# Batch 1 of a fused attention and FFN kernel: projections one step sooner, q turned one or two steps sooner, score groups moved to two and one steps later

## The chip, the cores and the metric

The kernel runs on one core of one Trainium2 chip. A core has five engines that run their own instruction streams and meet at semaphores: PE (matrix multiply, with PEld for its weight loads), DVE (VectorE), ACT (ScalarE), POOL (GpSimd) and SP (SyncE). PE, DVE, ACT, POOL and SP execute their instructions in the order in which the program gives them; DMA transfers are issued by SP, ACT and POOL and run on 16 DMA engines. The metric is device time in microseconds, the median of several runs.

## The reference

Linformer attention for 8 batches of 8 heads, 1024 rows, head size 64, followed by a feed-forward network whose hidden layer is the maximum of three products:

```python
k_proj = np.einsum('ks,bhsd->bhkd', E, k)          # E, F: 64 x 1024
v_proj = np.einsum('ks,bhsd->bhkd', F, v)
scores = scale * np.matmul(q, k_proj.transpose(0, 1, 3, 2))
attn = softmax(scores)                              # over 64 columns
x = np.matmul(attn, v_proj)  -> (8192, 512)
h = np.maximum(np.maximum(x @ w1, x @ w2), x @ w3)  # 512 -> 768
out = h @ w_out                                     # 768 -> 512
```

Softmax is written there with the row maximum subtracted; the kernel computes the exponentials, their sums (by a product with ones) and the reciprocal as exp(-ln(sum)).

## The kernel before

The weights stay in the on-chip memory. Everything is worked out batch by batch: the attention of batch b + 1 is put between the steps of the FFN of batch b, by hand. All of PE's results go to one PSUM tile `ps` of eight banks: banks 0 to 3 rotate through the FFN (`fbank`), banks 4 to 7 belong to the attention.

**The FFN.** A batch has two halves (`ch`) of 512 tokens. A half has 18 layer-1 steps (`l1`): for each of six blocks of hidden units the products with w1, w2 and w3, four matmuls of 128x512 each (L188). ScalarE copies the first product to `h1s` (L191), VectorE takes the maximum with the second into `m12` (L193) and with the third into `hT` (L195). Then come four `down` steps (L212) of six matmuls, a ScalarE copy (L214) and a store from POOL (L219).

**Steps and groups.** After each step `tick()` counts `slot` up and calls the groups of the next batch's attention whose slot is reached. Groups stand in a list, in the order in which they are called. In batch 0 the first half is special (`l1_first`, `down_half`: slots 1 to 16), the second half gives slots 17 to 34 (one per layer-1 step), and its four down steps slots 35 to 38. So step 20 here is the layer-1 step that brings `slot` to 20; steps 17, 20, 23, 26, 29, 32 are those with the ScalarE copy.

**The attention of batch 1** has these groups:

- `g1[0]`, kv: 16 matmuls project k and v (L119, L121) into bank 4; ScalarE casts the result to `kp` (L126), VectorE repeats it (L127), SP issues a transposing DMA from `kp` to `kpT` (L176), ScalarE and VectorE write `vp` (L129, L130).
- `q_flip(1, 0..3)`: VectorE turns q, two heads at a time, from `q_t` to `qT` (L99).
- `g1[1]`, `g1[2]`, scores: 32 small matmuls each (L140) of `kpT` with four heads of `qT` into banks 4 to 7, then two exponentials on ScalarE into `pT` (L145), four banks in a call. Both groups use the same four banks, and each fills half of the columns twice over (gg = 0 and 1).
- `g1[3]`, sums: 16 matmuls of `pT` with ones (L154) and two logarithms (L161); `g1[4]`, `g1[5]`: reciprocals (L164); `g1[6]`, `g1[7]`: the products of `pT` with `vp` (L154), which VectorE multiplies by the reciprocals into `xT` (L169), the FFN's input.

**The loads.** POOL issues k, v and q of batch 1 early (L417 to L419); they run behind the weights. At slot 22 of batch 0 `load_behind_turn(2, "kvq")` makes POOL copy one element of `kpT` (L91), which waits for the transposing DMA, and then issues the loads of batch 2 (L87).

The other batches use the list that `attention` returns (kv at 2, scores at 10 and 15, sums at 20, and so on); batch 1 has the list of its own that the change touches.

Of the kernel before, what the change touches and what calls it, by code (L numbers as in the profile page):

```python
# [16 lines left out]
def kernel(ctx: ExitStack, tc: tile.TileContext, q, k, v, E, F, w1, w2, w3, w_out, out):  # L17
# [71 lines left out]
    def load_behind_turn(b, order="qkv"):  # L89

        nc.gpsimd.tensor_copy(out=seen, in_=kpT[(b - 1) % NB][:, 0, 0, 0:1])  # L91
        for c in order:
            load(b, *{"q": (q, q_t), "k": (k, k_t), "v": (v, v_t)}[c])
# [3 lines left out]
    def q_flip(b, g):  # L97
        hs = slice(2 * g, 2 * g + 2)
        nc.vector.transpose(  # L99
            out=qT[b % NB][:, hs].bitcast(FP32).rearrange("p h n -> p (h n)"),  # L100
            in_=q_t[b % NB][:, hs].rearrange("p h si d -> p (h si d)").bitcast(FP32),
        )
# [82 lines left out]
    def l1(b, ch, c, jt, i):  # L185
        bank = fbank()
        for ct in range(NCT):
            nc.tensor.matmul(out=ps[:, bank, :], lhsT=w_sb[i][:, ct, jt * P:(jt + 1) * P],  # L188
                             rhs=xT[b % 2][:, ct, ch, :], start=(ct == 0), stop=(ct == NCT - 1))
        if i == 0:  # L190
            nc.scalar.copy(out=h1s[jt % 2], in_=ps[:, bank, :])  # L191
        elif i == 1:
            nc.vector.tensor_tensor(out=m12[jt % 2], in0=ps[:, bank, :], in1=h1s[jt % 2], op=ALU.max)  # L193
        else:
            nc.vector.tensor_tensor(out=hT[c % 2][:, jt, :], in0=ps[:, bank, :], in1=m12[jt % 2], op=ALU.max)  # L195

    def down(b, ch, c, tt):
        o = o_acc[c % 2]
        if c == 2 * B - 1 and tt == 3:

            n = DO // 2
            for x, tmp in enumerate(h1s):
                bank = fbank()
                for jt in range(NJT):
                    nc.tensor.matmul(out=ps[:, bank, :n], lhsT=hT[c % 2][:, jt, tt * P:(tt + 1) * P],
                                     rhs=wo_sb[:, jt, x * n:(x + 1) * n], start=(jt == 0), stop=(jt == NJT - 1))
                (nc.scalar.copy if x else nc.vector.tensor_copy)(out=tmp[:, :n], in_=ps[:, bank, :n])
                (nc.scalar if x else nc.sync).dma_start(out=out_v[b, ch][:, tt, x * n:(x + 1) * n], in_=tmp[:, :n])
            return
        bank = fbank()  # L210
        for jt in range(NJT):
            nc.tensor.matmul(out=ps[:, bank, :], lhsT=hT[c % 2][:, jt, tt * P:(tt + 1) * P],  # L212
                             rhs=wo_sb[:, jt, :], start=(jt == 0), stop=(jt == NJT - 1))
        nc.scalar.copy(out=o[:, tt, :], in_=ps[:, bank, :])  # L214
        if c == 2 * B - 1:
            nc.sync.dma_start(out=out_v[b, ch][:, tt, :], in_=o[:, tt, :])
        elif tt % 2 == 1:
            dst = out_v[b, ch] if b else out_0[ch]
            nc.gpsimd.dma_start(out=dst[:, tt - 1:tt + 1, :], in_=o[:, tt - 1:tt + 1, :])  # L219

    def down_half(tt, x):

        bank = tt
        for jt in range(3 * x, 3 * x + 3):
            nc.tensor.matmul(out=ps[:, bank, :], lhsT=hT[0][:, jt, tt * P:(tt + 1) * P],  # L225
                             rhs=wo_sb[:, jt, :], start=(jt == 0), stop=(jt == NJT - 1))
        if x:
            nc.scalar.copy(out=o_acc[0][:, tt, :], in_=ps[:, bank, :])
            if tt % 2 == 1:
                nc.gpsimd.dma_start(out=out_0[0][:, tt - 1:tt + 1, :], in_=o_acc[0][:, tt - 1:tt + 1, :])  # L230


    def quads0(ch, bank, lhs, hhs=(0, 1)):
        for hh, j, g, u in QUADS:
            if hh not in hhs:
                continue
            rows = slice(u * KP, (u + 1) * KP)
            nc.tensor.matmul(out=ps[j * HD:(j + 1) * HD, bank + hh, :], lhsT=lhs(rows, g),  # L238
                             rhs=pT[rows, g, ch, :], start=True, stop=True, tile_position=(u * KP, j * HD))
# [24 lines left out]
    def sums0(ch, bank):  # L264
        quads0(ch, bank, lambda rows, g: ones[rows, :])
        nc.scalar.activation(out=lns[ch], in_=ps[:, bank:bank + 2, :], func=AF.Ln)
        nc.scalar.activation(out=rinv[ch], in_=lns[ch], func=AF.Exp, scale=-1.0)
# [30 lines left out]
    def av_up0():  # L298
        for f, bank in enumerate((6, 4)):
            quads0(1, bank, lambda rows, g: vp2[0][rows, g, f, :])  # L300
        norm0(1, 0, 6, (0, 1))
        norm0(1, 1, 4, (0, 1))
# [96 lines left out]
    def l1_first(i, jts, banks, between=None):  # L399
        for hh in range(2):  # L400
            if hh and between:
                between()
            for jt, bank in zip(jts, banks):
                for ct in (2 * hh, 2 * hh + 1):
                    nc.tensor.matmul(out=ps[:, bank, :], lhsT=w_sb[i][:, ct, jt * P:(jt + 1) * P], rhs=xT[0][:, ct, 0, :],  # L405
                                     start=(ct == 0), stop=(ct == NCT - 1))
                if hh:
                    nc.vector.tensor_tensor(out=h1c[jt] if i == 1 else hT[0][:, jt, :], in0=ps[:, bank, :], in1=h1c[jt],
                                            op=ALU.max)
                    yield  # L410
# [35 lines left out]
    for b in range(B):  # L446
        groups = attention(b + 1, turn_dma) if b + 1 < B else []
        if b == 0:
            g1 = [g for _, g in groups]
            groups = [(9, scores_up0), (12, lambda: sums0(1, 4)), (20, g1[0]),  # L450
                      (22, lambda: q_flip(1, 0)), (23, lambda: q_flip(1, 1)), (25, g1[1]), (26, lambda: q_flip(1, 2)),
                      (27, lambda: q_flip(1, 3)), (28, g1[2]),
                      (31, g1[3]), (32, g1[4]), (33, g1[5]), (34, g1[6]), (36, g1[7])]
        slot = 0
        gi = 0

        def tick():
            nonlocal slot, gi
            slot += 1
            while gi < len(groups) and groups[gi][0] <= slot:  # L460
                groups[gi][1]()
                gi += 1
            if b == 0:
                if slot == 22:
                    load_behind_turn(2, "kvq")
                return
            if b == 1 and slot in (4, 5, 6, 7):
                q_flip(2, slot - 4)
            if b + 2 < B:
                if slot == 9:  # L470
                    load_behind_turn(b + 2)
                if slot in (32, 34, 36, 38):
                    q_flip(b + 2, slot // 2 - 16)

        for ch in range(2):
            c = 2 * b + ch
            if c == 0:
                for part in ((1, range(6), (6, 7, 0, 1, 4, 5)), (2, range(3), (2, 3, 0), q_up0), (2, range(3, 6), (1, 2, 3))):
                    for _ in l1_first(*part):
                        tick()  # L480
                state["f"] = 3
                for x in range(2):
                    if x:
                        av_up0()
                    for tt in range(4):
                        down_half(tt, x)
                        if x:
                            tick()
                continue
            for s in range(18):  # L490
                l1(b, ch, c, s // 3, s % 3)
                tick()
                if pend and s in (2, 5, 8, 11):
                    pend.pop(0)()
                    tick()
            pend = [lambda tt=tt, b=b, ch=ch, c=c: down(b, ch, c, tt) for tt in range(4)]
        if b == 0:
            while pend:
                pend.pop(0)()
                tick()  # L500
# [32 lines left out]
```

The softmax here doesn't subtract the row's maximum and nothing guards it: scores larger than these inputs give would overflow.

## Time and profile before

| | |
|---|---|
| median of 8 runs | 400.9 us (400.51 to 401.11) |
| the profiled execution | 400.91 us |
| its span, first to last instruction | 399.0 us |
| PE busy | 388.1 us, 97% of the span, 2686 instructions |
| DVE busy | 200.2 us, 50% |
| ACT busy | 163.5 us, 41% |
| POOL busy | 66.6 us, 17% |
| chain that ended last | PE 92%, DVE 3%, DMA 2%, issue 1%, ACT 1% |

A busy PE counts the length of overlapping matmuls, so 97% says that PE seldom stands still and not how fast it works. The page's slices give the granted TensorE clock as 9 in all 40 of them, and its mean is 1.000. The stretch from 44.98 us (the first layer-1 matmul of batch 0's second half) to 73.21 us (the first of batch 1) is the one in which batch 1's attention is worked in. Busy time of the engines there, by stage:

| from to, us | what PE does | PE busy | DVE busy | ACT busy |
|---|---|---|---|---|
| 44.98 to 48.53 | steps 17 to 20 | 3.55 | 1.05 | 1.31 |
| 48.53 to 50.38 | kv | 1.85 | 0.33 | 0.58 |
| 50.38 to 55.51 | steps 21 to 25 | 4.44 | 4.15 | 1.53 |
| 55.51 to 58.79 | first scores, steps 26 to 28 | 3.23 | 1.41 | 2.42 |
| 58.79 to 63.11 | second scores, steps 29 to 31 | 3.49 | 1.89 | 2.42 |
| 63.11 to 66.37 | sums, steps 32 to 34 | 3.21 | 1.40 | 2.57 |
| 66.37 to 69.62 | product with vp, steps 35 and 36 | 3.25 | 3.15 | 2.33 |
| 69.62 to 73.21 | product with vp, steps 37 and 38 | 3.38 | 2.74 | 1.17 |

### The profile page before, as it was taken

The numbers are of one execution on the slowest core, as the hardware profiler recorded it, in microseconds if no ns is written. First come the engines' busy times: TensorE is split into PE (matmuls) and PEld (weight loads), VectorE is DVE, ScalarE is ACT, GpSimd is POOL, SyncE is SP. The second block draws the span as 40 slices with busy tenths as digits, with TensorE's granted clock in tenths as the row PEclk, the third lists the DMA queues.
The fourth block names the chain that finished last, engine by engine and source line by source line (L and its number), as shares of the span: only waits on it lengthen the run. The fifth ranks groups of instructions, "written<-read, shape, count | busy, mean of one in ns | idle before, by whom it ended". The sixth has DMA issues, their size and how long they took to land.

```text
span 399.0 us, 6581 instructions
## 1 busy us (share of the span) xinstructions
PE 388.1 (97%) x2686; PEld 171.6 (43%) x2736; DVE 200.2 (50%) x295; ACT 163.5 (41%) x247; POOL 66.6 (17%) x110
## 2 busy tenths in 40 slices
PE   7999989999999999999999999999999999999996
PEld 4444433444444444444444444444444444444443
DVE  2447365573853367443863267442674338433341
ACT  3413437337234642347223662245523472222222
POOL 6452141150003300050000600032000000000000
PEclk9999999999999999999999999999999999999999
DMA  8999979879213982259511991139912211102022
GB/s 223 206 209 206 206 173 192 205 114 204 74 53 84 194 174 95 38 112 206 160 53 28 177 221 78 54 80 187 183 53 70 64 54 53 55 19 86 2 105 105
DMA packets 41293, 48.39 MB, mean 121 GB/s; under 512 B 9136, under 2 KB 36272, under 8 KB 41264
## 3 DMA queue, kind: packets, MB, share of 16 engines
q0 software_dynamic: 31776, 43.52, 52.7%
q1 hardware_dynamic: 8656, 3.54, 4.4%
q10 hardware_dynamic: 832, 0.92, 0.7%
q8 instruction: 21, 0.34, 0.3%
q14 instruction: 8, 0.07, 0.1%
HBM read 57.15 MB, written 16.78 MB: 185 GB/s over the span
## 4 chain that ended last, share of the span: by engine, by line
PE 92%; DVE 3%; DMA 2%; issue 1%; ACT 1%; POOL 0%; DVEq 0%; POOLq 0%
PE ps L188 57%; PE ps L212 19%; PE ps L119 3%; PE ps L154 3%; DMA k_t<-in_k_dram 2%; PE ps L405 2%; PE ps L140 2%; PE ps L396 1%; PE ps L225 1%; PE ps L306 1%; PE ps L238 1%; DVE xT L169 1%; PE ps L258 1%; DVE m L193 0%; ACT pT L145 0%
## 5 line engine op out<-in xcount | busy, mean ns | idle before, releaser
L188 PE MATMUL ps<-xT,w_sb 128*128 128x512 bf16 x1043 | 243.8, 379 | 1.9
L188 PEld LDWEIGHTS <-w_sb 128*128 128x128 bf16 x1080 | 103.3, 98 | 130.8 <-issue 10.2
L193 DVE TENSOR_TENSOR m<-ps,h1s 128x512 f32<-128x512 f32 x90 | 62.1, 690 | 135.1 <-PE ps L188 108.2
L212 PE MATMUL ps<-wo_sb,hT 128*128 128x512 bf16 x348 | 85.0, 379 | 0.5 <-issue 0.2
L191 ACT COPY h1s<-ps 128x512 f32<-128x512 f32 x90 | 52.9, 587 | 67.3 <-PE ps L188 67.3
L214 ACT COPY o_acc<-ps 128x512 f32<-128x512 f32 x59 | 34.6, 586 | 100.6 <-PE ps L212 100.6
L195 DVE TENSOR_TENSOR hT<-ps,m 128x512 bf16<-128x512 f32 x90 | 61.8, 687 | 12.2 <-PE ps L188 5.2
L219 POOL DMA_DIRECT2D out_dram<-o_acc x28 | 15.2, 544 | 275.1 <-ACT o_acc L214 266.1
L212 PEld LDWEIGHTS <-hT 128*128 128x128 bf16 x354 | 33.6, 98 | 43.0 <-issue 4.4
L169 DVE TENSOR_TENSOR xT<-ps,rinv 128x1024 bf16<-128x1024 f32 x28 | 32.9, 1217 | 7.5 <-PE ps L154 7.5
L145 ACT ACTIVATE pT<-ps 128x1024 bf16<-128x1024 f32 x28 | 27.1, 1021 | 19.5 <-PE ps L140 17.0
L99 DVE STREAM_TRANSPOSE qT<-q_t 128x512 f32<-128x512 f32 x28 | 19.3, 695 | 0.0
L87 POOL DMA_DIRECT2D v_t<-in_v_dram x21 | 15.3, 761 | 4.1 <-DMA w_sb<-in_moe_w_dram 2.2
L161 ACT ACTIVATE lns<-ps 128x1024 f32<-128x1024 f32 x14 | 13.6, 1021 | 1.7 <-PE ps L154 1.7
L164 ACT ACTIVATE rinv<-lns 128x1024 f32<-128x1024 f32 x14 | 14.2, 1061 | 0.0
L119 PE MATMUL ps<-k_t,eT 128*64 128x512 bf16 x56 | 13.4, 382 | 0.0
L121 PE MATMUL ps<-v_t,fT 128*64 128x512 bf16 x56 | 13.4, 382 | 0.0
L87 POOL DMA_DIRECT2D q_t<-in_q_dram x14 | 10.6, 769 | 3.2 <-DMA wo_sb<-in_moe_w_out_dram 1.1
L140 PE MATMUL ps<-qT,kpT 32*64 32x256 bf16 x448 | 9.5, 277 | 1.5 <-DVE qT L99 0.8
L87 POOL DMA_DIRECT2D k_t<-in_k_dram x14 | 10.6, 769 | 1.9 <-issue 1.4
L405 PE MATMUL ps<-xT,w_sb 128*128 128x512 bf16 x46 | 10.6, 379 | 0.2 <-issue 0.2
L306 PE MATMUL ps<-warm 128*128 128x512 bf16 x23 | 8.8, 474 | 1.5 <-DVE ones L338 1.2
(82 smaller groups left out, 150.3 us busy)
## 6 DMA issues: line engine op xcount, KB each, us to landing
out_dram<-o_acc POOLq DMA_DIRECT2D x30, 512.0 KB, 2.9
q_t<-in_q_dram POOLq DMA_DIRECT2D x15, 512.0 KB, 8.9
k_t<-in_k_dram POOLq DMA_DIRECT2D x14, 512.0 KB, 11.5
v_t<-in_v_dram POOLq DMA_DIRECT2D x18, 256.0 KB, 15.2
v_t<-in_v_dram POOLq DMA_DIRECT2D x7, 512.0 KB, 14.8
w_sb<-in_moe_w_dram POOLq DMA_DIRECT2D x4, 384.0 KB, 10.1
k_t<-in_k_dram POOLq DMA_DIRECT2D x4, 256.0 KB, 9.2
w_sb<-in_moe_w_dram POOLq DMA_DIRECT2D x4, 192.0 KB, 9.1
```

The costliest lines, as they stand in the source:

```text
L87: nc.gpsimd.dma_start(out=dst[b % NB][:, slots], in_=sv[:, heads])
L99: nc.vector.transpose(out=qT[b % NB][:, hs].bitcast(FP32).rearrange("p h n -> p (h n)"), in_=q_t[b % NB][:, hs].rearrange("p h si d -> p ( ...
L119: nc.tensor.matmul(out=ps[0:KP, AB, :], lhsT=eT[:, si, :], rhs=k_t[i][:, :, si, :], start=(si == 0), stop=(si == SI - 1))
L145: nc.scalar.activation(out=pT[:, 2 * u + gg].rearrange("p ch (t r n) -> p r (ch t) n", t=4, r=4), in_=ps[:, AB:AB + 4, gg * 256:(gg + 1) * ...
L169: nc.vector.tensor_tensor(out=xT[b % 2][:, 2 * u + half, :, :], in0=ps[:, AB + 2 * u:AB + 2 * u + 2, :], in1=rinv[u].rearrange("p (c n) -> ...
L188: nc.tensor.matmul(out=ps[:, bank, :], lhsT=w_sb[i][:, ct, jt * P:(jt + 1) * P], rhs=xT[b % 2][:, ct, ch, :], start=(ct == 0), stop=(ct == ...
L191: nc.scalar.copy(out=h1s[jt % 2], in_=ps[:, bank, :])
L193: nc.vector.tensor_tensor(out=m12[jt % 2], in0=ps[:, bank, :], in1=h1s[jt % 2], op=ALU.max)
L195: nc.vector.tensor_tensor(out=hT[c % 2][:, jt, :], in0=ps[:, bank, :], in1=m12[jt % 2], op=ALU.max)
L212: nc.tensor.matmul(out=ps[:, bank, :], lhsT=hT[c % 2][:, jt, tt * P:(tt + 1) * P], rhs=wo_sb[:, jt, :], start=(jt == 0), stop=(jt == NJT - 1))
L214: nc.scalar.copy(out=o[:, tt, :], in_=ps[:, bank, :])
L405: nc.tensor.matmul(out=ps[:, bank, :], lhsT=w_sb[i][:, ct, jt * P:(jt + 1) * P], rhs=xT[0][:, ct, 0, :], start=(ct == 0), stop=(ct == NCT ...
```

## The change

Only the list of batch 1's groups is edited. Each number is the slot behind which a group is called.

```diff
-            groups = [(9, scores_up0), (12, lambda: sums0(1, 4)), (20, g1[0]),
-                      (22, lambda: q_flip(1, 0)), (23, lambda: q_flip(1, 1)), (25, g1[1]), (26, lambda: q_flip(1, 2)),
-                      (27, lambda: q_flip(1, 3)), (28, g1[2]),
+            groups = [(9, scores_up0), (12, lambda: sums0(1, 4)), (19, g1[0]),
+                      (21, lambda: q_flip(1, 0)), (22, lambda: q_flip(1, 1)), (24, lambda: q_flip(1, 2)),
+                      (25, lambda: q_flip(1, 3)), (27, g1[1]), (29, g1[2]),
                       (31, g1[3]), (32, g1[4]), (33, g1[5]), (34, g1[6]), (36, g1[7])]
```

| group | slot before | slot after |
|---|---|---|
| kv | 20 | 19 |
| q_flip 0, 1 | 22, 23 | 21, 22 |
| q_flip 2, 3 | 26, 27 | 24, 25 |
| first scores | 25 | 27 |
| second scores | 28 | 29 |
| sums and later | 31 to 36 | 31 to 36 |

All four turns of q now stand ahead of the first scores. No instruction is added or removed. The order of instructions on POOL and SP stays as it was; on PE, DVE and ACT the groups move past the FFN's instructions between their old and new slots. On ACT, kv's two casts go ahead of the `h1s` copy of step 20, and the first exponentials go behind that of step 26.

## The prediction

> **What bounds the kernel now.** I read the shares first: PE is busy for 97% of the span and holds 92% of the chain that ended last, so only what lets PE stand still can be won or lost. Next the list of waits, for PE alone. Over the whole span it has eight rows; restricted to 73 us and later it is empty. After batch 1, then, PE is never released late, and a microsecond won or lost before 73 us should reach the end whole. Two of the eight rows lie in the region of the change, both before the score matmuls of L140:
>
> ```profile
> PE ps L140 <- DVE qT L99: 0.8, 1, 0.8
> PE ps L140 <- DMA kpT<-kp: 0.6, 1, 0.6
> ```
>
> The timeline of PE shows the places (start, length, instruction, idle time before it and its releaser):
>
> ```profile
> 44.98 3.62 PE L188 MATMUL ps<-xT,w_sb 128*128 128x512 bf16 x16
> 48.53 0.40 PE L119 MATMUL ps<-k_t,eT 128*64 128x512 bf16 x1
> ...
> 50.38 4.49 PE L188 MATMUL ps<-xT,w_sb 128*128 128x512 bf16 x19
> 55.51 0.66 PE L140 MATMUL ps<-qT,kpT 32*64 32x256 bf16 x32 [0.64 <-DMA kpT<-kp]
> 56.10 2.76 PE L188 MATMUL ps<-xT,w_sb 128*128 128x512 bf16 x11
> 58.79 0.43 PE L140 MATMUL ps<-qT,kpT 32*64 32x256 bf16 x16
> 60.06 0.43 PE L140 MATMUL ps<-qT,kpT 32*64 32x256 bf16 x16 [0.83 <-DVE qT L99]
> 60.42 2.76 PE L188 MATMUL ps<-xT,w_sb 128*128 128x512 bf16 x12
> 63.11 0.63 PE L154 MATMUL ps<-pT,ones 64*32 64x512 bf16 x16
> ```
>
> Matmuls overlap, so I count from start to start. The same pieces without a stall stand in batch 2:
>
> ```profile
> 83.89 0.66 PE L140 MATMUL ps<-qT,kpT 32*64 32x256 bf16 x32
> 84.48 4.49 PE L188 MATMUL ps<-xT,w_sb 128*128 128x512 bf16 x19
> 88.91 0.66 PE L140 MATMUL ps<-qT,kpT 32*64 32x256 bf16 x32
> ```
>
> A score group costs 0.59 (84.48 - 83.89), twenty L188 matmuls 4.43 (by the code 20; one record is missing), twelve 2.69 (63.11 - 60.42). So one more matmul costs (4.43 - 2.69)/8 = 0.217, a step of four 0.87, and two steps ahead of a group 2.69 - 0.87 = 1.82.
>
> **What the change takes away.** First stall: L188 runs from 50.38, so the scores could start at 54.81; they start at 55.51: 0.70. Second: 58.79 to 60.42 is 1.63 against 0.59: 1.04. Together 1.74 us. Both causes get room:
> - Projections (kv). One step sooner they start at 44.98 + 3.55 - 0.87 = 47.66. Their last input is v's last part, issued at 31.5 and 15.3 on its way: 46.8. In time, by 0.9.
> - What kv issues: ScalarE's cast of kp (50.51 before) at 49.64, VectorE's copy at 50.26, the transpose DMA at 50.84 (51.70 before; SP has nothing else). It took 3.8 us: landing 54.6.
> - The q turns now stand on VectorE behind L193 of step 21 and alternate with the FFN's own 0.69 us operations: about 52.1, 53.4, 54.7 and 55.9, 0.70 each. The two halves of q land at 33.1 + 16.3 = 49.4 and 35.0 + 16.9 = 51.9, before the turn that needs each. The last ends at 56.6. L193 and L195 finish behind a turn at the latest by 57.3, and the four FFN banks they free are asked for a step or more later, so PE doesn't notice.
> - First scores: kv ends at 49.52, eight steps are 4.43 + 12 x 0.217 = 7.03, so they start at **56.54**, 1.9 after the transpose. The second scores would start at 56.54 + 0.59 + 1.82 = 58.95, the sums at 61.37; the last turn at 56.6 is early for both.
>
> A rule that speaks against moving the transpose forward: the Trainium skill, "DMA: Bandwidth & Descriptors", section "Queues, rings and completion order", has each DMA engine alternate between queues packet by packet, draining a packet of one before it turns to the next. The sooner transpose falls on the tail of q's load and an output store, which keep the DMAs full to about 52.5. By the row (3.8) it lands at 54.6; if the rule let none of it run before that tail is gone, it would land no later than now, about 55.5, since its packets begin at 52.5 in the trace of before. The sum is the same: 56.54 is later than both. I take 54.6 and keep 55.5.
>
> **What the change adds.** The score groups now stand two steps apart (three before), and the sums two steps after the second (three before). Each group's exponentials on ScalarE lie between:
>
> ```profile
> 89.64 1.94 ACT L145 ACTIVATE pT<-ps 128x1024 bf16<-128x1024 f32 x2 [1.77 <-PE ps L140]
> ```
>
> The scores of that row started at 88.91; ScalarE was idle and began 0.73 later, when all 32 matmuls were done. From the start of scores to the end of both exponentials is 0.73 + 1.94 = 2.67; with 0.05 for the release (the transposes of qT end at 60.01, PE goes on at 60.06) 2.72. In the built program the first matmul of the second scores waits for both exponentials of the first (same four banks), and the first matmul of the sums for both of the second. PE arrives after 0.59 + 1.82 = 2.41. So each place stalls for 2.72 - 2.41 = **0.31**, twice: 0.61 (unrounded). Before, a third step covered this (0.87 more room). ScalarE is free in time: the h1s copy of step 26 ends at 56.4, the scores are ready at 57.3; that of step 29 runs at 59.1 to 59.7, the second scores are ready at 59.26 + 0.73 = 59.99. Waiting behind a stalled group on PE are the FFN steps, and behind the sums ln, the reciprocals and L169.
>
> Bounds of this added wait: the trace of before never shows the two so close. At the low end 0, were PE to run on while ScalarE reads; at the high end 1.2, were ScalarE's h1s copy (0.58) to come in front of one group's exponentials (0.61 + 0.58). I take 0.61, because the two exponentials with their lag are the same in every undisturbed batch.
>
> **What stays.** From the sums on, order and steps are unchanged: ln at 63.80 is 0.69 behind the sums at 63.11, then reciprocals, L169, second attention product. Its stall (start to start 1.22 at 69.62 against 0.55 at 66.37, so 0.67) hangs on that ScalarE and VectorE chain, which starts at the sums, and moves with it. The sums start at 56.54 + 2 x 2.72 = 61.98 instead of 63.11: **1.13 us sooner**, which is 1.74 - 0.61.
>
> POOL's small copy waits for the transpose, and behind it stand batch 2's loads and two stores; it runs up to 0.86 sooner. The consumers come 1.13 sooner, so margin shrinks by 0.3, or by 1.1 if the transpose lands as before. Batch 2's v lands at 59.0 + 11.8 = 70.8 and is used at 75.03; the second half of q lands at 60.4 + 16.1 = 76.5, its turns come after 79.3. Both margins are wider, so it costs nothing; a cover gone would cost what it exceeds.
>
> **Sum.** The profiled execution took 400.91 us with a span of 399.0, so 1.9 lies around the span and is untouched. 400.91 - 1.13 = 399.8, span 397.9. The median of the eight runs is 400.9, the same. A change under 0.2% (0.8 us) is about what a measurement of this kernel can't tell from none.
>
> **Rivals.**
> - *The exponentials don't bind* (PE overlaps them): all of 1.74 comes, 399.2. For it: the excess is only 0.31 at each place. Against: one ScalarE runs them in order, and its row leaves no room. 0.12.
> - *No gain to be told*: the added waits take their high end of 1.2 or more, or later work gives the gain back; 400.4 to 400.9. For it: three engines must pass work within two steps. Against: PE's list is empty after 73 us. 0.13.
> - *Slower*: the transpose, now among the loads, is held longer than the tail explains. Each microsecond of landing beyond 56.54 is on the path; the change turns slower from 56.54 + 1.13 = 57.67, when the transpose takes 6.8 instead of 3.8. At double time (7.6) it lands at 58.4: 1.9 stall, 0.8 net loss, 401.7. For it: it is the only transpose that meets other traffic, and took 3.8 against 3.5. Against: the loads are over by 51.9. 0.09.
>
> **How the numbers follow.** The forecast's case has 0.66, of which 0.05 could fall under the 0.8 us. Faster: 0.61 + 0.12 = 0.73; same: 0.05 + 0.13 = 0.18; slower 0.09. The forecast with its added wait between 0 and 1.2 spans 399.2 to 400.4, and run-to-run scatter (400.51 to 401.11) adds some 0.2 below; upward I reach to 400.6 to hold part of the no-gain case.
>
> **What would show it.** In the profile after: no wait of L140 for kpT or L99; instead L140 and L154 each wait once, about 0.3 us, for ACT pT L145; scores at 56.5 and 59.3, sums at 62.0; the second attention product still resumes 7.0 after the sums start; span near 397.9. Wrong would be: a kpT wait at the first scores, a wait at L119 for v, scores 2.4 apart without a wait, or new rows for PE after 73 us.

## The result and the profile after

The changed kernel takes 399.05 us in the median of 11 runs (398.66 to 400.53), against 400.83 for 32 runs of the kernel before. The ratio is 0.9959, 95% interval 0.9952 to 0.9967. Of 400.83 that ratio is 1.64 us less (1.3 to 1.9); the two medians differ by 1.78. The forecast was 1.13 less, 399.8, so 399.05 stands at the low end of what it allowed (399.2 to 400.4, and some 0.2 of scatter below). The profiled execution took 398.9, with a span of 397.0.

The list of PE's waits, changed kernel, whole span (who waited for whom, total, times, longest):

```profile
PE ps L306 <- DVE ones L338: 1.2, 1, 1.2
PE ps L244 <- DVE qT L357: 0.3, 1, 0.3
PE ps L140 <- ACT pT L145: 0.2, 1, 0.2
PE ps L154 <- ACT pT L145: 0.2, 1, 0.2
```

The two waits of L140 for kpT and for the turned q are gone, and two waits for the exponentials stand in their place, one before the second scores and one before the sums. Another row is gone that the change doesn't touch: the wait of L244 for k at the start of the kernel (1.5 us). The timeline of PE in the region, changed kernel:

```profile
43.91 2.75 PE L188 MATMUL ps<-xT,w_sb 128*128 128x512 bf16 x12
46.59 0.40 PE L119 MATMUL ps<-k_t,eT 128*64 128x512 bf16 x1
46.84 0.38 PE L121 MATMUL ps<-v_t,fT 128*64 128x512 bf16 x1
...
48.66 7.08 PE L188 MATMUL ps<-xT,w_sb 128*128 128x512 bf16 x31
55.67 0.66 PE L140 MATMUL ps<-qT,kpT 32*64 32x256 bf16 x32
56.26 1.90 PE L188 MATMUL ps<-xT,w_sb 128*128 128x512 bf16 x7
58.39 0.66 PE L140 MATMUL ps<-qT,kpT 32*64 32x256 bf16 x32 [0.23 <-ACT pT L145]
58.98 1.90 PE L188 MATMUL ps<-xT,w_sb 128*128 128x512 bf16 x8
61.11 0.63 PE L154 MATMUL ps<-pT,ones 64*32 64x512 bf16 x16 [0.23 <-ACT pT L145]
```

Read the score groups first. They start at 55.67 and 58.39, 2.72 apart, and the sums at 61.11, again 2.72 later: that is the forecast's whole round trip, and 0.31 more than the 2.41 that PE needs for a group and two steps. (The list says 0.2, since it counts idle time from the modelled end of the last matmul.) Then read the first line: step 17 starts at 43.91, not at 44.98. So 1.07 of the 2.00 us by which the spans differ was there before any moved instruction. From step 17 to the sums it is 17.20 here and was 18.13 (63.11 - 44.98), a difference of 0.93. The forecast had 17.00; the missing 0.2 is in kv, where L121 starts 0.25 behind L119 instead of beside it, and kv takes 2.07 (46.59 to 48.66) instead of 1.85. v's last part was issued at 31.2 and landed 15.5 later, at 46.7, just behind kv's start. In every other trace kv starts at 46.83 or later, behind v's landing, and takes 1.85.

That leaves a riddle. If the early start were luck, the medians should differ by 1.13 or less; they differ by more. The answer is in the transpose of kp. Its rows, first of the kernel before, then of the changed one (length of the issuing instruction in ns, time of issue; then the time from issue to landing):

```profile
L176 SPq DMA_TRANSPOSE kpT<-kp x1: 1402/1402/1402, 51.7 to 51.7; - x1
...
DMA to landing us min/median/max: 3.8/3.8/3.8
```

```profile
L176 SPq DMA_TRANSPOSE kpT<-kp x1: 1313/1313/1313, 50.0 to 50.0; - x1
...
DMA to landing us min/median/max: 5.5/5.5/5.5
```

It was issued 1.7 sooner and landed at the same time: 51.7 + 3.8 = 55.5 and 50.0 + 5.5 = 55.5. What the DMAs did between 52 and 54 us of the changed kernel's span, by queue (packets, MB, and the time that the packets took as a share of 16 engines' time, which can pass 100%; q1 is the transpose, q0 the transfers that POOL issues, here the end of batch 0's two stores):

```profile
q1 hardware_dynamic: 483, 0.12, 101.6%
q0 software_dynamic: 83, 0.27, 32.8%
```

The transpose has 1056 packets, so less than half of them moved here. By single microseconds it was 375 from 52 to 53, 108 from 53 to 54, and the other 573 from 54 to 55, when the stores were done.

**Theory T1:** kpT lands when the tail of loads and stores lets it, near 55.4 us, whatever PE does. In the kernel before, the first scores hang on it, so an early start of PE is lost there in a longer wait. In the changed kernel they stand behind it, and an early start comes through to the end. **Rival T2:** the transpose takes some 3.8 us from its issue and moves with PE, as the forecast took it; the extra gain is an early start that either kernel can have.

### The profile page after: what moved, and what is told of

Read it like the earlier page. It is cut to its first block, busy times and chain, and to the rows that moved or that the text cites. A ratio compares the mean times of both kernels' runs of the same rounds, so it can differ in the third digit from the quotient of the medians.

```text
span 397.0 us, 6579 instructions
## 1 busy us (share of the span) xinstructions
PE 388.3 (98%) x2686; PEld 172.0 (43%) x2736; DVE 200.3 (50%) x295; ACT 163.5 (41%) x247; POOL 66.5 (17%) x110
## 4 chain that ended last, share of the span: by engine, by line
PE 96%; issue 1%; ACT 1%; DVE 1%; DVEq 0%
PE ps L188 58%; PE ps L212 19%; PE ps L154 3%; PE ps L119 3%; PE ps L405 3%; PE ps L140 2%; PE ps L306 2%; PE ps L396 1%; PE ps L225 1%; ACT pT L145 1%; PE ps L238 1%; DVE xT L169 1%; PE ps L258 1%; PE ps L346 1%; PE ps L121 0%
## 5 line engine op out<-in xcount | busy, mean ns | idle before, releaser
L119 PE MATMUL ps<-k_t,eT 128*64 128x512 bf16 x56 | 13.4, 382 | 0.0
L121 PE MATMUL ps<-v_t,fT 128*64 128x512 bf16 x56 | 13.4, 382 | 0.0
L126 ACT CAST kp<-ps 64x512 bf16<-64x512 f32 x7 | 4.0, 578 | 16.1 <-PE ps L121 16.1
```

The source lines that it names most:

```text
L119: nc.tensor.matmul(out=ps[0:KP, AB, :], lhsT=eT[:, si, :], rhs=k_t[i][:, :, si, :], start=(si == 0), stop=(si == SI - 1))
```

## The experiments

**The kernel before once more, and kv alone.** The first is unchanged. The second has one number edited:

```diff
-            groups = [..., (20, g1[0]),
+            groups = [..., (19, g1[0]),
```

> The kernel before, unchanged, for a second trace. Theory T1 (the transpose of kp lands when the loads' and stores' tail lets it, near 55.4 us, whatever PE does): first scores start at 55.5 again, even if the first L188 of step 17 starts anywhere between 43.9 and 45.0. Rival T2 (the transpose takes 3.8 us from its issue and so moves with PE; the extra gain was an early start that either kernel can have): first scores start 10.5 us behind that L188, that is 54.5 if it starts at 43.9.

> kv alone at slot 19, all else as before. T1: kpT still lands near 55.4, first scores at 55.5, time as before (within 0.3 us). T2: the transpose lands 0.87 sooner, the first stall of 0.70 goes: 0.7 us less than before.

The repeated kernel before, timeline of PE:

```profile
43.71 3.62 PE L188 MATMUL ps<-xT,w_sb 128*128 128x512 bf16 x16
...
49.11 4.49 PE L188 MATMUL ps<-xT,w_sb 128*128 128x512 bf16 x20
55.09 0.66 PE L140 MATMUL ps<-qT,kpT 32*64 32x256 bf16 x32 [1.49 <-DMA kpT<-kp]
...
62.69 0.63 PE L154 MATMUL ps<-pT,ones 64*32 64x512 bf16 x16
```

This time step 17 started 1.27 us sooner than in the first trace, and the first scores only 0.42 sooner, at 55.09; T1 asks for 55.5 and T2 for 54.2. The wait for kpT grew from 0.64 to 1.49 and ate the rest. The execution took 400.36 (one run). kv alone gives 400.76, ratio 1.0 (0.9991 to 1.0008), where T2 had 0.7 less: its transpose was issued at 50.7, took 4.5, and the first scores started at 55.17. T2 falls on both. T1's landing was put 0.3 to 0.4 too late; from here on it is 55.1 to 55.5.

**The turns alone.** kv at 20 and scores at 25 and 28 as before, only q turned sooner:

```diff
-  (22, lambda: q_flip(1, 0)), (23, lambda: q_flip(1, 1)), (25, g1[1]), (26, lambda: q_flip(1, 2)),
-  (27, lambda: q_flip(1, 3)), (28, g1[2]),
+  (21, lambda: q_flip(1, 0)), (22, lambda: q_flip(1, 1)), (24, lambda: q_flip(1, 2)), (25, lambda: q_flip(1, 3)),
+  (25, g1[1]), (28, g1[2]),
```

> q turned at slots 21, 22, 24, 25 as in the changed kernel, kv at 20 and scores at 25 and 28 as before. T1 and T2 alike: the second stall (1.04) goes, the first stays: 1.0 us less than before; second scores near 58.8, sums near 62.1, no wait for ACT pT. Under T1 first scores at 55.5 whatever the start.

399.75 us, ratio 0.9977 (0.9969 to 0.9985): 0.9 us less. Timeline of PE of this kernel:

```profile
55.32 0.66 PE L140 MATMUL ps<-qT,kpT 32*64 32x256 bf16 x32 [1.20 <-DMA kpT<-kp]
55.91 2.76 PE L188 MATMUL ps<-xT,w_sb 128*128 128x512 bf16 x12
58.61 0.66 PE L140 MATMUL ps<-qT,kpT 32*64 32x256 bf16 x32
```

The wait for kpT stays, the wait for q is gone, and with three steps between the groups nothing waits for ScalarE. So a little over half of the gain of 1.64 is the turns.

**The tail taken away from the kernel before.** The two stores of batch 0's first half go behind batch 2's loads on POOL:

```diff
 def down_half(tt, x):
...
-            if tt % 2 == 1:
-                nc.gpsimd.dma_start(out=out_0[0][:, tt - 1:tt + 1, :], in_=o_acc[0][:, tt - 1:tt + 1, :])
...
                     load_behind_turn(2, "kvq")
+                    for t0 in (0, 2):
+                        nc.gpsimd.dma_start(out=out_0[0][:, t0:t0 + 2, :], in_=o_acc[0][:, t0:t0 + 2, :])
```

> The kernel before with the two stores of batch 0's first half issued behind batch 2's loads, so that the tail ends with q at 51.9. T1: the transpose lands at 54.2 to 55.2, first scores up to 1.0 sooner (0.3 with a late start), 0.3 to 1.0 us less than before. T2: it takes 3.5 instead of 3.8 at best, 0 to 0.3 us less.

400.15 us, ratio 0.9986 (0.998 to 0.9993): 0.6 us less. The transpose was issued at 51.1 and took 3.6; the first scores started at 54.70. T1's range holds the gain; T2's end of 0.3 is just touched by the interval (0.3 to 0.8), and a landing 3.6 behind the issue suits both, so this run alone hardly parts them. Nothing on PE, DVE or ACT was moved, only two stores out of the transpose's way, and the landing follows the issue again.

**A delay put into both kernels.** Four matmuls whose result nobody reads go ahead of step 17:

```diff
+            if c == 1:
+                warmup(4, 7)
             for s in range(18):
```

> The kernel before with four idle matmuls of 128x512 (0.87 us of PE) ahead of step 17. T1 (kpT lands near 55.1 to 55.5 by the DMAs' own pace): PE's wait before the first scores takes the delay up, 0 to 0.3 us more than before. T2 (the transpose moves with PE): 0.87 us more.

> The changed kernel with the same four idle matmuls. T1: PE is no longer held at the first scores, so the delay shows: 0.65 to 0.87 us more than the changed kernel (0.2 of it can hide in kv's wait for v), a gain over before of about 0.9 instead of 1.6. T2: 0.87 more, as in the kernel before.

The kernel before with them: 400.96, ratio to the one without 1.0008 (0.9999 to 1.0016), so at most 0.6 of the 0.87 shows and 0.3 is likeliest. The changed kernel with them: 399.94, ratio to the kernel before 0.9983 (0.9976 to 0.9989) instead of 0.9959, that is 0.9 to 1.0 us more than without. The same delay is mostly hidden in one kernel and whole in the other, as T1 has it. The trace of the delayed changed kernel is also the forecast's own case, for its step 17 starts about where the forecast had it:

```profile
45.13 2.75 PE L188 MATMUL ps<-xT,w_sb 128*128 128x512 bf16 x12
...
49.66 7.08 PE L188 MATMUL ps<-xT,w_sb 128*128 128x512 bf16 x31
56.67 0.66 PE L140 MATMUL ps<-qT,kpT 32*64 32x256 bf16 x32
...
62.12 0.62 PE L154 MATMUL ps<-pT,ones 64*32 64x512 bf16 x16 [0.23 <-ACT pT L145]
```

62.12 - 45.13 is 16.99; the forecast's was 17.00.

**kv back at 20 in the changed kernel.**

```diff
-            groups = [..., (19, g1[0]),
+            groups = [..., (20, g1[0]),
```

> The changed kernel with kv back at slot 20. T1: kpT lands at the same time, near 55.4, and the first scores come to the same point: as the changed kernel or up to 0.2 us less, since kv no longer waits for v. The prediction on record counted a part of the 0.70 for kv's step; with the scores at 27 it gives the same time too.

399.04 us, ratio to the kernel before 0.9963 (0.9951 to 0.9976): the same as the changed kernel. Its transpose, issued at 50.9, took 4.2 and landed at 55.2; the first scores started at 55.75 without a wait. Moving kv is worth nothing that these runs can tell, alone (above) or with the rest. Since kv counts for nothing, the changed kernel and the one with the turns alone differ by the score slots: 399.05 against 399.75, with intervals that just don't overlap (0.9952 to 0.9967, 0.9969 to 0.9985). So the rest of the gain, some 0.7 us, is the slots. The slots without the sooner turns were not run.

**Looking for a better place.** With the stores late, kpT lands sooner, so the scores can go back to 25 and 28, where three steps cover the exponentials:

```diff
-                      (25, lambda: q_flip(1, 3)), (27, g1[1]), (29, g1[2]),
+                      (25, lambda: q_flip(1, 3)), (25, g1[1]), (28, g1[2]),
```

> kv at 19, q turned as in the changed kernel, scores back at 25 and 28, and batch 0's two stores behind batch 2's loads. T1: kpT lands at 53.8 to 54.4 behind q's last part, first scores there, no wait for ACT pT, sums near 60.9: 0.2 to 0.6 us less than the changed kernel. T2: transpose in 3.5, landing 53.5, first scores at 53.9: 0.6 less.

398.50 us (398.47 to 399.0), ratio to the kernel before 0.995 (0.9938 to 0.9963). PE's list has no wait of L140 or L154 left:

```profile
44.83 2.75 PE L188 MATMUL ps<-xT,w_sb 128*128 128x512 bf16 x12
...
54.65 0.66 PE L140 MATMUL ps<-qT,kpT 32*64 32x256 bf16 x32
...
57.93 0.66 PE L140 MATMUL ps<-qT,kpT 32*64 32x256 bf16 x32
...
61.22 0.62 PE L154 MATMUL ps<-pT,ones 64*32 64x512 bf16 x16
```

From step 17 to the sums it is 16.39, against 17.20 in the changed kernel, or 16.99 where kv doesn't wait for v. The trace is one with a late start, and of its kernel's five runs one of the two longer ones (398.92 and 399.0; the others 398.47 to 398.50). By medians it is the best version, 0.55 below the changed one, but the two intervals against the kernel before overlap (0.9938 to 0.9963 and 0.9952 to 0.9967). Three more kernels ask what it owes to what: the stores late with the changed kernel's slots; its slots with the stores in their old place; and the stores late with scores at 26 and 29. Their edits are those shown, with these numbers.

> The changed kernel with batch 0's two stores behind batch 2's loads. T1: kpT lands a microsecond sooner (near 54.3), but the first scores stand at slot 27 and come no sooner: as the changed kernel (within 0.3 us). The stores alone are then worth nothing here. T2: the same.

> e8 with the stores in their old place: kv at 19, turns as in the changed kernel, scores at 25 and 28. T1: first scores held to 55.1 to 55.5 by kpT, no wait for ACT pT: as e3, 399.7 to 399.9. T2: as e8, 398.5, since the transpose would land at 54 by itself.

> Stores late, kv at 19, scores at 26 and 29, sums at 31. First scores one step later than in e8 and so free of kpT even with an early start, no wait before the second scores, one of 0.31 before the sums. T1 and T2: 0.3 us less than the changed kernel, within 0.3 of e8.

| kernel | median us | ratio to before | interval |
|---|---|---|---|
| stores late, scores 27 and 29 | 399.03 | 0.9964 | 0.9952 to 0.9977 |
| stores in place, scores 25 and 28 | 399.66 | 0.9974 | 0.9965 to 0.9984 |
| stores late, scores 26 and 29 | 398.97 | 0.9957 | 0.9944 to 0.9969 |
| stores late, scores 25 and 28 | 398.50 | 0.9950 | 0.9938 to 0.9963 |

Late stores alone are worth nothing to the changed kernel, since its first scores stand behind the landing anyway. The old slots alone run into the landing again; the second kernel's list of PE's waits has

```profile
PE ps L140 <- DMA kpT<-kp: 1.2, 1, 1.2
```

and its time is that of the turns alone, as T1 says and T2 (398.5) doesn't. Both together give the lowest median and the shortest stretch from step 17 to the sums (16.39, against 16.99 with late stores alone and 61.84 - 44.15 = 17.69 with the old slots alone); by the times, whose intervals overlap, it is likely and not shown. The 0.3 us that the third kernel was to gain on the changed one doesn't show in its median, nor is it within 0.3 of the best one; in its trace the sums start 16.70 behind step 17 (60.97 - 44.27), 0.3 less than in the first kernel of the table (61.23 - 44.24 = 16.99).

All transposes of batch 1 side by side, from the rows of L176 and of PE's timelines. The landing is the start of POOL's small copy behind it (L91); the last store packet is that of q0 in slices of 0.05 us.

| kernel | step 17 starts | transpose issued | last store packet | landed | first scores |
|---|---|---|---|---|---|
| before | 44.98 | 51.7 | 54.05 | 55.52 | 55.51 |
| before, again | 43.71 | 50.4 | 53.65 | 55.10 | 55.09 |
| kv alone | 44.81 | 50.7 | 53.75 | 55.18 | 55.17 |
| turns alone | 44.23 | 51.0 | 53.90 | 55.33 | 55.32 |
| before, delayed | 44.76 | 51.5 | 53.75 | 55.20 | 55.19 |
| scores 25 and 28, stores in place | 44.15 | 50.0 | 53.85 | 55.28 | 55.27 |
| changed | 43.91 | 50.0 | 54.00 | 55.47 | 55.67 |
| changed, delayed | 45.13 | 51.0 | 53.75 | 55.20 | 56.67 |
| kv back at 20 | 44.21 | 50.9 | 53.75 | 55.21 | 55.75 |
| before, stores late | 44.36 | 51.1 | moved behind | 54.70 | 54.70 |
| stores late, scores 25 and 28 | 44.83 | 50.7 | moved behind | 54.32 | 54.65 |
| stores late, scores 27 and 29 | 44.24 | 50.1 | moved behind | 53.75 | 55.79 |
| stores late, scores 26 and 29 | 44.27 | 50.1 | moved behind | 53.76 | 54.95 |

With the stores in place the landing keeps within 0.5 us while the issue moves by 1.7, and in all nine traces it comes 1.4 to 1.5 behind the last store packet; 448 to 499 of the transpose's 1056 packets have moved by then. With the stores away it is 3.6 behind the issue. T1 named loads and stores; it is the stores alone, for with them away kpT landed at 53.75, sooner than the 54.3 that T1 gave for late stores, though q's last part came in until 51.6. T1 also has an end: at an issue of 51.5 and 51.7 the transpose took 3.7 and 3.8, close to the free 3.6, so a still later PE should carry the landing along; no run goes there.

The spans say the same. In the five traces with before's turns and score slots, from the first scores to the end of the span it is 343.5 us each time, while from step 17 to the end it is between 353.8 and 354.9: the end follows the landing. In the four with the changed slots, from step 17 to the end it is 352.9 three times and 353.1 once (the one where kv waits for v): the end follows the start. So the changed kernel also takes over the scatter of the start: its 11 runs have spans from 396.6 to 398.4, where 41 runs of the kernel before lie between 398.6 and 398.9, and its slowest run, 400.53, gains next to nothing.

## Why the prediction was right, and which term was too small

- **PE sets the end, and a microsecond won before 73 us stays won.** Right: from 73 us on the changed kernel's PE list is empty too, and the sums moved by as much as the span (63.11 to 61.11, 399.0 to 397.0).
- **The second stall (1.04).** Right: the turns alone bring 0.9.
- **The added waits (0.31 twice).** Right within 0.01 in four traces (2.72 or 2.73 from group to group: the changed kernel, the delayed one, kv back at 20, the stores late). The rival in which the exponentials don't bind forecast about the right time, 399.2, but for a reason that the trace refutes. That 399.2 lies nearer to 399.05 than the forecast's 399.8 is luck.
- **The first stall (0.70) is the term that was mis-sized.** It was read off one execution as if it belonged to the kernel. It is the distance between a landing that the DMAs fix (55.1 to 55.5) and a PE that arrives at 53.5 to 54.8, depending on when step 17 starts (43.71 to 44.98 in the traces). Start to start it was 0.70 in the first trace of before and 55.09 - 49.11 - 4.43 = 1.55 in the second. The trace on which the sum was made was the latest start of all without a delay. With the middle of the starts seen without a delay (about 44.2) PE arrives at 54.0, so the stall is 1.1 to 1.5 instead of 0.70; the changed kernel's sums come at 44.2 + 17.0 = 61.2, and those of before at landing + 7.6 (63.11 - 55.51), that is 62.7 to 63.1: a gain of 1.5 to 1.9, which is what was measured (1.3 to 1.9).
- **The transpose (3.8 from its issue).** Wrong as taken: 5.5. The other bound, set beside it by the rule on the alternating queues, had it land no later than before, at about 55.5; it landed at 55.47. The reading under that bound was off, which makes the hit partly luck: in the trace of before the transpose's first packet moved at 52.95 and not at 52.5, 1.25 behind the issue, and with the stores away it is about 1.2 as well (51.1 to 52.3). So the start of its packets wasn't held there; in the changed kernel it was (50.0 to 52.2), and in both the second half came only behind the last store packet. The sum was the same for both, so the error did no harm in the changed kernel. But carried over to the kernel before, that bound says that its first scores can't follow an early PE, and this step was not taken.
- **kv one step sooner.** Counted among the causes that get room; it is worth nothing that the runs can tell, since what gives room is the scores' later slot. Its margin against v, given as 0.9, was gone with the early start: the 0.25 by which L121 waited for v is a small form of the wait for v that the forecast had named as a sign of being wrong. It cost 0.2 in this trace.
- **The slower side** (the transpose held beyond 56.54) didn't come, but the cover was thin: the scores started 0.2 behind the landing.

## What to carry to other kernels

A wait for a transfer has two sides. Before its size is taken from one trace, ask which of the two moves from run to run, and whether the transfer's landing follows its issue or the traffic in front of it; a second trace of the unchanged kernel tells. Where a landing is fixed by traffic, issuing sooner buys nothing: move the consumer behind it, or move the traffic (here two stores nobody waits for) out of its way. And when a producer and a consumer on two engines alternate through the same banks, add the whole round trip and compare it with the work between: it gave the size of the new waits here.

## What the runs showed of the hardware

The same transposing DMA took between 3.6 and 5.5 us to land, by whether two 512 KB stores were queued on the same DMA engines; issued 1.7 us sooner, it landed at the same time. The Trainium skill's page "DMA: Bandwidth & Descriptors", section "Queues, rings and completion order", has the engines alternate between queues packet by packet. That leaves room for a wait but gives no size for it; here the landing came 1.4 to 1.5 us behind the stores' last packet. The runs show that the stores hold the transpose up, not why its second half goes only behind them. Unexpected was also the start of the kernel: step 17 began between 43.71 and 44.98 us in executions of kernels that are alike up to there, while v's last part landed between 46.4 and 46.8. The starts fall into two groups that part in the first 10 us. In the three traces with a late step 17 (44.81 to 44.98, no delay put in) the first matmuls on k (L244) start at 10.10 to 10.27, in the ten others at 8.79 to 9.27. In the first trace of the kernel before they wait 1.35 us for k. In the two others they wait for nothing, but the matmuls ahead of them take longer: one of 128x512 takes 0.61 us where it takes 0.39 in the other traces, at a granted clock of 1.00 in both. What makes them longer stays open.
